# A stream of converted weights in an attention and gated-MLP kernel: fewer conversion passes, another order of stages, and high halves cast on GpSimd

## The chip, the cores and the metric

One core of a Trainium2 chip runs the whole kernel in one launch. The core has TensorE (matmuls, with a weight load that overlaps them), VectorE (DVE), ScalarE (ACT), GpSimd (POOL), a queue of DMA issues on SyncE (SP) and 16 DMA engines. The metric is the device time of an execution in microseconds. The kernel before takes 1339.32 us, the median of three runs (1336.44 to 1340.88).

## The reference

The weights are float64; the kernel reads them as pairs of 32-bit words and makes one float32 of each pair. The other inputs are float32. B, H, S, D are 4, 12, 448, 64; the model width is 768; the two MLPs have widths 1536 and 2048.

```
q_n, k_n = rmsnorm(q, g_q), rmsnorm(k, g_k)
attn = softmax(q_n @ k_n.T / sqrt(64))        # 48 heads of 448 x 448
x = (attn @ v), heads side by side            # 1792 x 768
x = ((x @ w_a) * (x @ w_b)) @ w_out           # 768 -> 1536 -> 768
h = x @ w_in                                  # 768 -> 2048
out = (max(h, 0) + alpha * min(h, 0)) @ w_out2   # 2048 -> 768
```

## The kernel before

**Four batches, four kinds of stage.** For each batch b there are the stages a (the two products with w_a and w_b and their elementwise product), y (w_out of the first MLP), h (w_in of the second, then the leaky activation) and o (w_out of the second, transposed back and stored). Activations lie transposed, features on partitions, 448 columns of a batch. Their order is a list (L584); before, it is `a0 y0 a1 y1 h0 o0 h1 o1 a2 y2 h2 a3 o2 y3 h3 o3`. Every value is kept as a sum of two float16 numbers, a high and a low half, and a product of two such values is three matmuls (`prod`, L725). A unit of weights is 768 x 128 (for o 512 x 128) and serves 18 (12) matmuls; one stage is 24 units for a, 12 for y, 16 for h and 24 for o.

**The weight stream.** `stream` (L599) lists the units in the order of use. At its first use a unit is loaded raw (`w_load`, 768 KB), made float32 (`w_convert`), scaled by a power of two that comes from a sum of squares over its chain (`w_scale`, a small matmul with ones adds over partitions), split into halves (`w_split`) and written to scratch in device memory; later uses reload the halves (384 KB). After each unit, `next_w` calls `advance`, which lets each of these steps run so many units ahead of the one in use: 9, 7, 7 and 3 before (L692), 4 for reloads. `w_convert` is one ScalarE pass and three or four VectorE passes; `w_split` is a ScalarE cast for the high half (L684) and a VectorE pass for the low half (L685). There are 76 first uses in all; 8 conversions and 4 splits are done before a0.

**Attention, woven in.** A step (`att_steps`, L536) makes scores, softmax and probabilities of two tiles of 128 rows; seven tiles make a pair of heads, six pairs a batch, 21 steps a batch. Batch 0 is worked before a0, in float32. Later batches use halves: `probs` (L464) casts the high half on ScalarE (L477), makes the low half on VectorE (L478) into a `p16` buffer and transposes both by DMA (L484); `pv` multiplies with v. `RATE` (L883) says how many steps fall into each stage; a stage a(b) begins when its batch's steps are done. A stage that is followed at once by the one that reads its result (`after`, L781) splits its outputs at its end; otherwise the splits become tasks, one a unit.

**Order.** The framework orders each engine's instructions by a planner's costs, with a few pinned to the order of the program; each engine then runs its list in order, and waits at an instruction whose inputs are not there. DMAs are issued in order by SP. PSUM for stage products has three buffers (`ps_m`).

Of the kernel before, what the change touches and what calls it, by code (L numbers as in the profile page):

```python
# [19 lines left out]
def attention_gated_mlps_kernel(  # L20
# [57 lines left out]
    k16 = acts.tile([KP, 2, 2 * KB, 2, D], F16, name="k16")  # L78
    p16 = [acts.tile([128, 2, KB, 128], F16, name=f"p16_{i}") for i in range(3)]
    stat = [acts.tile([128, 2, NI + 2 * KB], F32, name=f"stat{i}") for i in range(2)]  # L80
# [11 lines left out]
    al = const.tile([128, KF2], F32, name="al")  # L92
    alb = const.tile([128, KF2], F32, name="alb")
    cg = const.tile([128, 1], F32, name="cg")
    icg = const.tile([128, 1], F32, name="icg")
    ncg = const.tile([128, 1], F32, name="ncg")
    ssv = const.tile([KP, B, NP], F32, name="ssv")
# [63 lines left out]
    def setup2():  # L161
        nc.gpsimd.dma_start(out=gbc, in_=g_q.rearrange("(o d) -> o d", o=1).broadcast_to([128, D]))
        nc.gpsimd.dma_start(out=gkb, in_=g_k.rearrange("(o d) -> o d", o=1).broadcast_to([128, D]))
        nc.gpsimd.dma_start(out=al, in_=alpha.rearrange("(f p) -> p f", p=128))
        nc.gpsimd.tensor_scalar(al, al, -1.0, None, op0=ALU.mult)

# [17 lines left out]
    def setup4():  # L184

        q = sm_p.tile([128, KF2], F32, tag="al2", name="al2")
        nc.vector.tensor_tensor(q, al, al, op=ALU.mult)
        m = sm_p.tile([128, 1], F32, tag="alm", name="alm")
        nc.vector.tensor_reduce(out=m, in_=q, axis=AX.X, op=ALU.max)
        t = total(m, 1)  # L190
        one = sm_p.tile([128, 1], F32, tag="alm", name="alo")
        nc.vector.tensor_scalar(one, t, 1.0, None, op0=ALU.max)
        power(one, cg, icg)
        nc.vector.tensor_scalar(cg, cg, 2.0 ** -31, None, op0=ALU.mult)
        nc.vector.tensor_scalar(ncg, cg, -1.0, None, op0=ALU.mult)
        nc.vector.tensor_scalar(icg, icg, 2.0 ** 31, None, op0=ALU.mult)
# [164 lines left out]
    def load_vn(b, p):  # L361
        vn = one_p.tile([KP, 2, KB, D], F32, tag="vn", name="vn")
        nc.sync.dma_start(
# [100 lines left out]
    def probs(m):  # L464
# [7 lines left out]
        for j in range(2):  # L472
# [3 lines left out]
            r = ri[:, j:j + 1]  # L476
            nc.scalar.activation(out=t[:, 0, :, 0:KP], in_=pf, func=AF.Copy, scale=r)  # L477
            nc.vector.scalar_tensor_tensor(  # L478
# [104 lines left out]

    stages = "a0 y0 a1 y1 h0 o0 h1 o1 a2 y2 h2 a3 o2 y3 h3 o3".split()  # L584

# [38 lines left out]
    def w_convert(u):  # L624
# [7 lines left out]
        ti = t.bitcast(I32)  # L632
        nc.scalar.activation(out=t, in_=hi.bitcast(F32), func=AF.Abs, scale=2.0 ** -112)  # L633
        i = nc.vector.tensor_scalar(ti, ti, 3, None, op0=ALU.logical_shift_left)
        if u == 0:
            tc.keep_in_program_order(i)
        nc.vector.scalar_tensor_tensor(  # L637
            out=ti, in0=hi, scalar=-0x80000000, in1=ti, op0=ALU.bitwise_and, op1=ALU.bitwise_or
        )
        nc.vector.scalar_tensor_tensor(  # L640
            out=ti, in0=lo, scalar=29, in1=ti, op0=ALU.logical_shift_right, op1=ALU.bitwise_or
        )
        if kind == "o":
# [6 lines left out]
            )  # L650
        wf[u] = t

    def w_scale(u):

        kind, n, part = stream[u]
        if u not in wf:
            return
        _, parts, _ = CHAINS[kind]
        chains = GROUP[kind]
        if part < parts - 1 or n % chains < chains - 1:  # L660
            return
        us = range(u - parts * chains + 1, u + 1)
        ss = sm_p.tile([128, 4], F32, tag="ss", name="ss")[:, 0:len(us)]
        sc = sm_p.tile([128, 2], F32, tag="sc", name="sc")[:, 0:chains]
        for i, x in enumerate(us):
            nc.scalar.activation(  # L666
                out=junk(768, size(kind)), in_=wf[x], func=AF.Square, accum_out=ss[:, i:i + 1]
            )
        power(total(ss, len(us), chains), sc, inv[kind][:, n - chains + 1:n + 1])
        for x in us:  # L670
# [7 lines left out]
    def w_split(u):  # L678
# [4 lines left out]
        w = wh_p.tile([128, 2, 768], F16, tag="w16", name="w16")[:, :, 0:n]  # L683
        nc.scalar.activation(out=w[:, 0], in_=t, func=AF.Copy, scale=s)  # L684
        nc.vector.scalar_tensor_tensor(  # L685
# [5 lines left out]

    STEPS = [(w_load, 9), (w_convert, 7), (w_scale, 7), (w_split, 3)]  # L692
    AGAIN = [(w_load, 4)]
# [127 lines left out]
    def stage_h(b):  # L821
        for f in range(KF2):
# [3 lines left out]
            for kk in range(KD):  # L826
                prod(ps, hw, kk, Y[b, kk], kk == 0, kk == KD - 1)
            next_w()
            t, t2 = tmp(), tmp()
            nc.scalar.activation(out=t, in_=ps, func=AF.Relu, scale=cg)  # L830
            nc.scalar.activation(out=t2, in_=ps, func=AF.Relu, scale=ncg)  # L831
            nc.vector.scalar_tensor_tensor(  # L832
                out=t, in0=t2, scalar=al[:, f:f + 1], in1=t, op0=ALU.mult, op1=ALU.add
            )
            G[b, f] = g = slot(f"g{b}_{f}")
            nc.vector.tensor_copy(g[:, 0], t)
            nc.vector.tensor_tensor(g[:, 1], t, g[:, 0], op=ALU.subtract)
        for kk in range(KD):
# [43 lines left out]

    RATE = {"a0": 15.5, "y0": 8, "a1": 8, "y1": 4, "h0": 3, "o0": 3, "h1": 5, "o1": 5, "a2": 9, "y2": 6, "h2": 9}  # L883

# [82 lines left out]
```

## Time and profile before

| | us |
|---|---|
| median of the runs | 1339.32 |
| profiled execution | 1339.62 |
| its span, first to last instruction | 1337.8 |
| TensorE busy (share) | 1203.4 (90%) |
| VectorE busy | 779.2 (58%) |
| ScalarE busy | 735.2 (55%) |
| GpSimd busy | 12.6 (1%) |
| mean granted TensorE clock | 0.945 of full |

A busy time is the union of an engine's instructions. TensorE's is modelled, since matmuls overlap, so its share does not say how near its peak it is. The engines wait for each other differently from stage to stage, so that the rows below cut the span into stages: each begins with the first matmul of that stage. The DMA share is the mean busy share of the 16 DMA engines. A wait is put down to whatever ended last before the waiting instruction began.

### The profile page before, as it was taken

The page shows a single profiled execution, that of the slowest core. Times are in us where ns is not written, and L with a number is a line of the kernel's source. Part 1 is how long each engine was busy: PE and PEld are TensorE (multiplying, and loading weights), DVE is VectorE, ACT ScalarE, POOL GpSimd, SP SyncE. Part 2 cuts the span into 40 slices and gives each one's busy share as a digit, 9 for nine tenths or more (in the row PEclk, how much of TensorE's full clock was granted, in tenths as well). Part 3 has the DMA queues.
Part 4 walks back from the last instruction along what each step waited for, and adds up shares of the span by engine and source line. Part 5 has one row for each costly group of instructions (what it writes and reads, how often), then busy time and mean ns, then how long its engine had stood idle before and what let it go on. Part 6 is the DMA issues. An engine that isn't in the chain of part 4 may idle for free. (4 is left out here: it accounts for less than half of the span.)

```text
span 1337.8 us, 18305 instructions
## 1 busy us (share of the span) xinstructions
PE 1203.4 (90%) x6574; PEld 611.7 (46%) x6574; DVE 779.2 (58%) x1639; ACT 735.2 (55%) x1480; POOL 12.6 (1%) x33
## 2 busy tenths in 40 slices
PE   6697887667898989988889999998999999999998
PEld 4353343333344545443445554554545555544554
DVE  6788889788888476999968833334045113003510
ACT  6698788778775577976755634444133113013310
POOL 1000000000000000000000000000000000000000
PEclk9798898877898989998999999998999999999999
DMA  4536999997999956967888667765423433543333
GB/s 106 187 103 184 248 260 256 236 252 203 246 259 268 245 144 194 250 200 214 237 222 208 142 158 200 173 158 120 115 95 119 118 112 104 150 125 95 106 117 91
DMA packets 324491, 234.67 MB, mean 175 GB/s; under 512 B 190992, under 2 KB 297744, under 8 KB 324400
## 3 DMA queue, kind: packets, MB, share of 16 engines
q1 hardware_dynamic: 324288, 233.43, 65.8%
q8 instruction: 52, 0.85, 0.3%
q0 software_dynamic: 112, 0.07, 0.1%
q14 instruction: 39, 0.32, 0.1%
HBM read 155.79 MB, written 32.24 MB: 141 GB/s over the span
## 5 line engine op out<-in xcount | busy, mean ns | idle before, releaser
L110 PEld LDWEIGHTS <-w 128*128 128x128 f16 x4896 | 480.8, 100 | 519.7 <-issue 71.0
L110 PE MATMUL p<-x,w 128*128 128x448 f16 x1728 | 347.0, 361 | 16.6 <-DVE w L685 9.6
L110 PE MATMUL p<-g,w 128*128 128x448 f16 x1152 | 232.8, 361 | 15.6 <-ACT w L684 11.6
L110 PE MATMUL p<-y,w 128*128 128x448 f16 x1152 | 224.6, 356 | 3.9 <-ACT y L739 3.6
L110 PE MATMUL p<-ab,w 128*128 128x448 f16 x864 | 172.7, 360 | 6.7 <-ACT ab L739 4.2
L110 PE MATMUL s<-kT,qT 128*64 128x448 f16 (+1 forms) x588 | 109.2, 416 | 26.8 <-ACT pf L434 19.5
L417 DVE TENSOR_REDUCE nm<-s 128x2 f32<-128x896 f32 x84 | 91.2, 1085 | 35.6 <-PE s L110 35.1
L478 DVE SCALAR_TENSOR_TENSOR p<-pf,ri,p 128x448 f16<-128x448 f32 x126 | 83.3, 680 | 42.1 <-ACT p L477 41.9
L477 ACT ACTIVATE p<-pf,ri 128x448 f16<-128x448 f32 x126 | 80.3, 662 | 37.7 <-DMA pT<-p 32.9
L434 ACT ACTIVATE pf<-s,nm,esc 128x448 f32<-128x448 f32 x126 | 90.0, 718 | 2.7 <-DVE p L478 1.0
L761 DVE SCALAR_TENSOR_TENSOR ab<-p,inv_a,t 128x448 f32<-128x448 f32 x48 | 32.6, 679 | 94.0 <-PE p L110 93.7
L857 DVE TENSOR_SCALAR ob<-p,cum 112x512 f32<-112x512 f32 x24 | 18.0, 749 | 116.8 <-PE p L855 108.1
L848 ACT ACTIVATE t<-p,inv_o 128x448 f32<-128x448 f32 x24 | 25.6, 1067 | 107.3 <-PE p L110 107.3
L633 ACT ACTIVATE wf<-raw 128x768 f32<-128x768 f32 (+1 forms) x76 | 63.0, 831 | 37.3 <-DMA raw<-in_moe_w_out_dram 21.9
L830 ACT ACTIVATE t<-p,cg 128x448 f32<-128x448 f32 x64 | 40.3, 629 | 76.2 <-PE p L110 73.6
L832 DVE SCALAR_TENSOR_TENSOR t<-t,al 128x448 f32<-128x448 f32 x64 | 43.6, 681 | 56.1 <-ACT t L831 56.1
L685 DVE SCALAR_TENSOR_TENSOR w<-wf,sc,w 128x768 f16<-128x768 f32 (+1 forms) x76 | 70.2, 926 | 0.3 <-ACT w L684 0.3
L764 ACT ACTIVATE junk<-ab 128x448 bf16<-128x448 f32 x48 | 27.4, 572 | 75.5 <-DVE ab L761 73.2
L666 ACT ACTIVATE junk<-wf 128x768 bf16<-128x768 f32 (+1 forms) x76 | 58.8, 773 | 15.6 <-DVE wf L646 8.9
L684 ACT ACTIVATE w<-wf,sc 128x768 f16<-128x768 f32 (+1 forms) x76 | 63.2, 860 | 6.1 <-DVE sc L120 6.1
L637 DVE SCALAR_TENSOR_TENSOR wf<-raw,wf 128x768 int32<-128x768 int32 (+1 forms) x76 | 65.8, 866 | 0.2
L640 DVE SCALAR_TENSOR_TENSOR wf<-raw,wf 128x768 int32<-128x768 int32 (+1 forms) x76 | 65.8, 866 | 0.2
(134 smaller groups left out, 1080.3 us busy)
## 6 DMA issues: line engine op xcount, KB each, us to landing
w<-sc_a SPq DMA_DIRECT2D x72, 384.0 KB, 3.3
w<-sc_h SPq DMA_DIRECT2D x48, 384.0 KB, 3.1
w<-sc_o SPq DMA_DIRECT2D x72, 256.0 KB, 3.0
w<-sc_y SPq DMA_DIRECT2D x36, 384.0 KB, 3.1
raw<-in_moe_w_in_dram SPq DMA_DIRECT2D x16, 768.0 KB, 6.1
raw<-in_moe_w_out_dram SPq DMA_DIRECT2D x24, 512.0 KB, 3.9
raw<-in_moe_w_a_dram SPq DMA_DIRECT2D x12, 768.0 KB, 5.7
raw<-in_moe_w_b_dram SPq DMA_DIRECT2D x12, 768.0 KB, 5.6
```

The costliest lines, as they stand in the source:

```text
L110: nc.tensor.matmul(out=o, lhsT=a, rhs=b, start=first, stop=last)
L417: nc.vector.tensor_reduce(out=nm, in_=ps[:, :, 0:S], axis=AX.X, op=ALU.max, negate=True)
L434: nc.scalar.activation(out=pf, in_=ps[:, j, 0:S], func=AF.Exp, bias=nm[:, j:j + 1], scale=scale[j], accum_out=su[:, j:j + 1],)
L477: nc.scalar.activation(out=t[:, 0, :, 0:KP], in_=pf, func=AF.Copy, scale=r)
L478: nc.vector.scalar_tensor_tensor(out=t[:, 1, :, 0:KP], in0=pf, scalar=r, in1=t[:, 0, :, 0:KP], op0=ALU.mult, op1=ALU.subtract,)
L633: nc.scalar.activation(out=t, in_=hi.bitcast(F32), func=AF.Abs, scale=2.0 ** -112)
L637: nc.vector.scalar_tensor_tensor(out=ti, in0=hi, scalar=-0x80000000, in1=ti, op0=ALU.bitwise_and, op1=ALU.bitwise_or)
L640: nc.vector.scalar_tensor_tensor(out=ti, in0=lo, scalar=29, in1=ti, op0=ALU.logical_shift_right, op1=ALU.bitwise_or)
L666: nc.scalar.activation(out=junk(768, size(kind)), in_=wf[x], func=AF.Square, accum_out=ss[:, i:i + 1])
L684: nc.scalar.activation(out=w[:, 0], in_=t, func=AF.Copy, scale=s)
L685: nc.vector.scalar_tensor_tensor(out=w[:, 1], in0=t, scalar=s, in1=w[:, 0], op0=ALU.mult, op1=ALU.subtract)
L832: nc.vector.scalar_tensor_tensor(out=t, in0=t2, scalar=al[:, f:f + 1], in1=t, op0=ALU.mult, op1=ALU.add)
```

## The change

The order of stages becomes `a0 y0 h0 o0 a1 y1 a2 h1 o1 y2 a3 h2 y3 o2 h3 o3`, with other rates of attention steps (4 in a0, 14 in a1). `w_convert` takes the sign along in the ScalarE pass (Prelu with a negative slope of a power of two, in place of Abs) and so drops the VectorE pass that joined the sign. The squares of a unit are summed at the end of `w_convert`, and `w_scale` only adds the totals; the lookaheads become 10, 8, 6 and 3. `w_split` and `probs` cast the high half on GpSimd instead of ScalarE; there are four `p16` buffers for three. Stage h uses one Relu on ScalarE and a VectorE pass that reads PSUM again, then the common `split`, in place of two Relus, a VectorE pass, a VectorE copy and a VectorE subtraction. The tile `vn` shares the pool of the output tiles.

```diff
--- before.py
+++ after.py
@@ -76,7 +76,7 @@
     kT0 = [kT0[:, i] for i in range(2)]
     kd0 = acts.tile([128, 2 * KB * D], F32, name="kd0")
     k16 = acts.tile([KP, 2, 2 * KB, 2, D], F16, name="k16")
-    p16 = [acts.tile([128, 2, KB, 128], F16, name=f"p16_{i}") for i in range(3)]
+    p16 = [acts.tile([128, 2, KB, 128], F16, name=f"p16_{i}") for i in range(4)]
     stat = [acts.tile([128, 2, NI + 2 * KB], F32, name=f"stat{i}") for i in range(2)]
 
     ident = const.tile([128, 128], F32, name="ident")
@@ -90,10 +90,8 @@
     gi = const.tile([128, 1], F32, name="gi")
     esc = const.tile([128, 1], F32, name="esc")
     al = const.tile([128, KF2], F32, name="al")
-    alb = const.tile([128, KF2], F32, name="alb")
     cg = const.tile([128, 1], F32, name="cg")
     icg = const.tile([128, 1], F32, name="icg")
-    ncg = const.tile([128, 1], F32, name="ncg")
     ssv = const.tile([KP, B, NP], F32, name="ssv")
     ssab = const.tile([128, 2, KF], F32, name="ssab")
     sx, ix, sab, iab, sy, iy, cum = [
@@ -162,7 +160,6 @@
         nc.gpsimd.dma_start(out=gbc, in_=g_q.rearrange("(o d) -> o d", o=1).broadcast_to([128, D]))
         nc.gpsimd.dma_start(out=gkb, in_=g_k.rearrange("(o d) -> o d", o=1).broadcast_to([128, D]))
         nc.gpsimd.dma_start(out=al, in_=alpha.rearrange("(f p) -> p f", p=128))
-        nc.gpsimd.tensor_scalar(al, al, -1.0, None, op0=ALU.mult)
 
     def setup3():
         tc.keep_in_program_order(
@@ -184,7 +181,7 @@
     def setup4():
 
         q = sm_p.tile([128, KF2], F32, tag="al2", name="al2")
-        nc.vector.tensor_tensor(q, al, al, op=ALU.mult)
+        tc.keep_in_program_order(nc.vector.tensor_tensor(q, al, al, op=ALU.mult))
         m = sm_p.tile([128, 1], F32, tag="alm", name="alm")
         nc.vector.tensor_reduce(out=m, in_=q, axis=AX.X, op=ALU.max)
         t = total(m, 1)
@@ -192,7 +189,7 @@
         nc.vector.tensor_scalar(one, t, 1.0, None, op0=ALU.max)
         power(one, cg, icg)
         nc.vector.tensor_scalar(cg, cg, 2.0 ** -31, None, op0=ALU.mult)
-        nc.vector.tensor_scalar(ncg, cg, -1.0, None, op0=ALU.mult)
+        nc.vector.tensor_scalar(al, al, -1.0, 1.0, op0=ALU.mult, op1=ALU.add)
         nc.vector.tensor_scalar(icg, icg, 2.0 ** 31, None, op0=ALU.mult)
 
 
@@ -359,7 +356,7 @@
         d["qT"], d["kT"] = qT, kT
 
     def load_vn(b, p):
-        vn = one_p.tile([KP, 2, KB, D], F32, tag="vn", name="vn")
+        vn = ob_p.tile([KP, 2, KB, D], F32, tag="ob", name="vn")
         nc.sync.dma_start(
             out=vn, in_=v[b, 2 * p:2 * p + 2].rearrange("h (p i) d -> p h i d", i=KB)
         )
@@ -474,7 +471,7 @@
             t = p16[(2 * m + j) % len(p16)]
             pf = pfs[j].rearrange("p (i j) -> p i j", i=KB)
             r = ri[:, j:j + 1]
-            nc.scalar.activation(out=t[:, 0, :, 0:KP], in_=pf, func=AF.Copy, scale=r)
+            nc.gpsimd.tensor_scalar(t[:, 0, :, 0:KP], pf, r, None, op0=ALU.mult)
             nc.vector.scalar_tensor_tensor(
                 out=t[:, 1, :, 0:KP], in0=pf, scalar=r, in1=t[:, 0, :, 0:KP],
                 op0=ALU.mult, op1=ALU.subtract,
@@ -581,7 +578,7 @@
             yield fin
 
 
-    stages = "a0 y0 a1 y1 h0 o0 h1 o1 a2 y2 h2 a3 o2 y3 h3 o3".split()
+    stages = "a0 y0 h0 o0 a1 y1 a2 h1 o1 y2 a3 h2 y3 o2 h3 o3".split()
 
     CHAINS = {"a": (2 * KF, 1, KD), "y": (KD, 2, KF // 2), "h": (KF2, 1, KD), "o": (KD, 4, KF2 // 4)}
 
@@ -630,13 +627,13 @@
         lo, hi = pair[:, :, 0], pair[:, :, 1]
         t = wf_p.tile([128, 768], F32, tag="wf", name="wf")[:, 0:size(kind)]
         ti = t.bitcast(I32)
-        nc.scalar.activation(out=t, in_=hi.bitcast(F32), func=AF.Abs, scale=2.0 ** -112)
+
+        nc.scalar.activation(
+            out=t, in_=hi.bitcast(F32), func=AF.Prelu, scale=2.0 ** -112, alpha=-(2.0 ** 32)
+        )
         i = nc.vector.tensor_scalar(ti, ti, 3, None, op0=ALU.logical_shift_left)
         if u == 0:
             tc.keep_in_program_order(i)
-        nc.vector.scalar_tensor_tensor(
-            out=ti, in0=hi, scalar=-0x80000000, in1=ti, op0=ALU.bitwise_and, op1=ALU.bitwise_or
-        )
         nc.vector.scalar_tensor_tensor(
             out=ti, in0=lo, scalar=29, in1=ti, op0=ALU.logical_shift_right, op1=ALU.bitwise_or
         )
@@ -649,24 +646,29 @@
                 op=ALU.mult,
             )
         wf[u] = t
+        _, parts, _ = CHAINS[kind]
+        j = (n * parts + part) % (parts * GROUP[kind])
+        if j == 0:
+            sums[0] = sm_p.tile([128, 4], F32, tag="ss", name="ss")
+        nc.scalar.activation(
+            out=junk(768, size(kind)), in_=t, func=AF.Square, accum_out=sums[0][:, j:j + 1]
+        )
+        if j == parts * GROUP[kind] - 1:
+            squares[u] = sums[0][:, 0:j + 1]
+
+    sums, squares = [None], {}
 
     def w_scale(u):
 
+        if u not in squares:
+            return
         kind, n, part = stream[u]
-        if u not in wf:
-            return
         _, parts, _ = CHAINS[kind]
         chains = GROUP[kind]
-        if part < parts - 1 or n % chains < chains - 1:
-            return
         us = range(u - parts * chains + 1, u + 1)
-        ss = sm_p.tile([128, 4], F32, tag="ss", name="ss")[:, 0:len(us)]
         sc = sm_p.tile([128, 2], F32, tag="sc", name="sc")[:, 0:chains]
-        for i, x in enumerate(us):
-            nc.scalar.activation(
-                out=junk(768, size(kind)), in_=wf[x], func=AF.Square, accum_out=ss[:, i:i + 1]
-            )
-        power(total(ss, len(us), chains), sc, inv[kind][:, n - chains + 1:n + 1])
+        iv = inv[kind][:, n - chains + 1:n + 1]
+        power(total(squares.pop(u), len(us), chains), sc, iv)
         for x in us:
             scales[x] = sc[:, (x - us[0]) // parts:(x - us[0]) // parts + 1]
 
@@ -681,7 +683,7 @@
         t, s = wf.pop(u), scales.pop(u)
         n = t.shape[1]
         w = wh_p.tile([128, 2, 768], F16, tag="w16", name="w16")[:, :, 0:n]
-        nc.scalar.activation(out=w[:, 0], in_=t, func=AF.Copy, scale=s)
+        nc.gpsimd.tensor_scalar(w[:, 0], t, s, None, op0=ALU.mult)
         nc.vector.scalar_tensor_tensor(
             out=w[:, 1], in0=t, scalar=s, in1=w[:, 0], op0=ALU.mult, op1=ALU.subtract
         )
@@ -689,7 +691,7 @@
         w16[u] = w
 
 
-    STEPS = [(w_load, 9), (w_convert, 7), (w_scale, 7), (w_split, 3)]
+    STEPS = [(w_load, 10), (w_convert, 8), (w_scale, 6), (w_split, 3)]
     AGAIN = [(w_load, 4)]
     cur = [0]
     seen = set()
@@ -826,15 +828,12 @@
             for kk in range(KD):
                 prod(ps, hw, kk, Y[b, kk], kk == 0, kk == KD - 1)
             next_w()
-            t, t2 = tmp(), tmp()
-            nc.scalar.activation(out=t, in_=ps, func=AF.Relu, scale=cg)
-            nc.scalar.activation(out=t2, in_=ps, func=AF.Relu, scale=ncg)
+            t = tmp()
+            nc.scalar.activation(out=t, in_=ps, func=AF.Relu, scale=-1.0)
             nc.vector.scalar_tensor_tensor(
-                out=t, in0=t2, scalar=al[:, f:f + 1], in1=t, op0=ALU.mult, op1=ALU.add
+                out=t, in0=t, scalar=al[:, f:f + 1], in1=ps, op0=ALU.mult, op1=ALU.add
             )
-            G[b, f] = g = slot(f"g{b}_{f}")
-            nc.vector.tensor_copy(g[:, 0], t)
-            nc.vector.tensor_tensor(g[:, 1], t, g[:, 0], op=ALU.subtract)
+            G[b, f] = split(t, cg, f"g{b}_{f}")
         for kk in range(KD):
             Y.pop((b, kk))
 
@@ -880,7 +879,7 @@
             G.pop((b, f))
 
 
-    RATE = {"a0": 15.5, "y0": 8, "a1": 8, "y1": 4, "h0": 3, "o0": 3, "h1": 5, "o1": 5, "a2": 9, "y2": 6, "h2": 9}
+    RATE = {"a0": 4, "y0": 5, "h0": 4, "o0": 8, "a1": 14, "y1": 7, "a2": 4, "h1": 4, "o1": 8, "y2": 6}
 
     if True:
         load_qk(0)
```

## Rows read from the trace of the kernel before

**Rows 1.** Stages: window, us, busy of PE, PEld, DVE, ACT, POOL, PEclk, DMA, GB/s

```profile
134.10:310.50 176.40, 129.31 (x684) 61.58 (x683) 149.01 (x294) 139.04 (x281) 0.56 (x1) 0.84 0.99 252
310.50:376.70 66.20, 60.28 (x333) 28.18 (x332) 58.06 (x123) 56.54 (x116) 0.27 (x1) 0.92 0.91 221
376.70:489.80 113.10, 104.20 (x586) 51.26 (x586) 77.27 (x167) 67.78 (x149) 2.24 (x4) 0.94 0.93 234
489.80:536.70 46.90, 46.90 (x270) 24.79 (x269) 31.50 (x59) 37.99 (x75) 0.00 (x0) 1.00 0.72 185
536.70:601.40 64.70, 60.46 (x327) 30.14 (x324) 64.31 (x127) 54.01 (x96) 2.02 (x3) 1.00 0.80 227
601.40:695.70 94.30, 78.03 (x387) 37.85 (x388) 82.15 (x172) 62.51 (x132) 0.00 (x0) 0.89 0.78 217
...
927.70:977.10 49.40, 47.21 (x247) 23.55 (x247) 9.50 (x19) 15.23 (x27) 0.42 (x3) 0.95 0.41 108
...
1033.10:1114.90 81.80, 81.80 (x435) 42.31 (x433) 9.23 (x14) 16.14 (x36) 0.00 (x0) 1.00 0.38 110
...
1173.80:1218.30 44.50, 42.33 (x224) 21.72 (x223) 1.75 (x6) 7.98 (x14) 0.39 (x2) 1.00 0.38 118
```

**Rows 2.** Stage a0, VectorE's maximum over scores (L417) alone

```profile
134.10:310.50 176.40, 16.24 (x15) 0.84 0.99 252
```

**Rows 3.** DMA issues in a1: count, KB each, us to landing

```profile
w<-sc_a SPq DMA_DIRECT2D x22, 384.0 KB, 5.0
raw<-in_moe_w_in_dram SPq DMA_DIRECT2D x6, 768.0 KB, 7.0
...
pT<-p SPq DMA_TRANSPOSE x18, 4.5
```

**Rows 4.** DMA issues in a3

```profile
w<-sc_a SPq DMA_DIRECT2D x20, 384.0 KB, 3.1
```

**Rows 5.** By line and shape: count | busy us, mean ns | idle before

```profile
L477 ACT ACTIVATE p<-pf,ri 128x448 f16<-128x448 f32 x126 | 80.3, 662 | 37.7 <-DMA pT<-p 32.9 <-ACT pf L434 2.4 <-issue 1.0
...
L685 DVE SCALAR_TENSOR_TENSOR w<-wf,sc,w 128x768 f16<-128x768 f32 x52 | 52.5, 1010 | 0.3 <-ACT w L684 0.3
...
L637 DVE SCALAR_TENSOR_TENSOR wf<-raw,wf 128x768 int32<-128x768 int32 x52 | 49.5, 951 | 0.2
L684 ACT ACTIVATE w<-wf,sc 128x768 f16<-128x768 f32 x52 | 47.6, 929 | 5.6 <-DVE sc L120 5.6
...
L837 DVE TENSOR_TENSOR g<-t,g 128x448 f16<-128x448 f32 x64 | 39.9, 623 | 1.4
...
L634 DVE TENSOR_SCALAR wf<-wf 128x768 int32<-128x768 int32 x52 | 28.6, 551 | 2.3 <-ACT wf L633 2.2
```

**Rows 6.** GpSimd in order of time: start us, us, operation

```profile
1.75 0.29 POOL masks.py:199 TENSOR_SCALAR_AFFINE_SELECT ident<-ident 128x128 f32<-128x128 f32 x1
1.99 0.84 POOL L146 MEMSET qT<- 128x896 f32 x1
...
380.54 0.47 POOL L812 TENSOR_TENSOR cum<-cum,iy 128x1 f32<-128x1 f32 x1 [69.77 <-DVE r L262]
381.08 0.96 POOL L813 TENSOR_TENSOR cum<-cum,icg 128x1 f32<-128x1 f32 x1
...
976.79 0.19 POOL L813 TENSOR_TENSOR cum<-cum,icg 128x1 f32<-128x1 f32 x1
```

**Rows 7.** VectorE in order of time, at the second of these

```profile
381.04 0.95 DVE L637 SCALAR_TENSOR_TENSOR wf<-raw,wf 128x768 int32<-128x768 int32 x1
```

**Rows 8.** Chain that ended last: start us, us, what

```profile
852.55 0.88 PE s L110 x8
853.43 10.32 PE p L110 x54
...
875.82 2.27 PE x L110 x24
```

**Rows 9.** ScalarE's table loads, by line

```profile
L237 ACT ACT_TABLE_LOAD x1 | 1.3, 1283 | 0.7 <-PEq L951 0.7
```

## The prediction

> **What bounds the kernel now.** I read the stage table first: the span cut where the first matmul of each stage starts. The reader is to see two halves. From h1 on TensorE is busy nearly all the time; a3 [rows 1] takes 81.8 us, and 24 chains of 18 products at 10.32/54 = 0.191 us a product [rows 8] are 82.5. Little is to be had there. In a0, y0, h0 and o0, the stages that convert weights, TensorE is not the limit: a0 lasts 176.4 us for 82.5 us of its own products. Its DMA share is 0.99, VectorE is busy 149.0 us and ScalarE 139.0 [rows 1]. So a0 goes at the pace of the DMA engines with VectorE next; h0 has VectorE at 64.3 of 64.7 us; o0 is near both (0.78 and 82.2 of 94.3). a1 is again near DMA, 0.93.
>
> **Prices of the DMA engines.** They are worked out from these shares, because the change moves no byte less, it only moves them elsewhere. a3: 0.38 x 81.8 = 31 us for 20 reloads of 384 KB and a few more [rows 1, 4], about 1.35 us each. a1: 0.93 x 113.1 = 105 us; 27 such reloads (22 of them the row shown) take 36, 6 raw loads of twice the size about 16, so the 18 probability transposes, 9 attention steps with the q, k, v that belong to them, take 53: 5.9 us a step [rows 1, 3, 4]. a0: 0.99 x 176.4 = 175; 15.5 steps [rows 2] take 91, which leaves 83 for 24 units, 3.5 us a unit (read and write-back); by size 2.35 for one of o.
>
> **The change on VectorE.** Conversion loses one of its passes, 0.951 us (0.63 for o, by size) [rows 5]. In h, three passes (one of them the 0.623 us subtraction [rows 5]) become two; about 0.3 us a tile, 5 us a stage. A step costs VectorE 3.5 us by what is left of a0's 149.0, 5.1 by what is left of a1's 77.3; I take 4.3. A conversion that stays is 0.55 + 0.95 = 1.5, a split 1.0 [rows 5].
> - a0: 149.0 - 24 x 0.95 - 11 steps x 4.3 = 79
> - y0: 58.1 - 4 x 4.3 + 7 conversions and 4 splits more, 14 - 5 lost passes, 5 + their totals, 2 = 52
> - h0: 64.3 + 3 x 4.3 + 5 conversions and 4 splits more, 12 - 11 lost passes, 9 - 5 = 75
> - o0: 82.2 + 2 x 4.3 - 19 lost passes, 12 - 3 conversions and 4 splits that moved forward, 8 = 71
>
> **The change on GpSimd.** It gets 72 weight casts and 42 probability casts in these four stages, and no GpSimd op of that shape is in the trace. Below: the memset, 0.84 us for 896 elements, 0.94 ns an element, so 0.42, 0.48 and 0.72 us for 448, 512 and 768. Above: the select, 0.29 us for 128 elements with all its cost charged per element, 2.25 ns, so 1.01, 1.15 and 1.73. Start-up is in the 128x1 op, 0.19 us when nothing disturbs it [rows 6]. I take start-up plus the memset's rate: 0.61, 0.67, 0.91, close to what ScalarE takes for them (0.66, 0.93 [rows 5]): 27 us in a0, 17 in y0, 17 in h0, 23 in o0.
>
> These casts are not free for VectorE. The same 128x1 op that takes 0.19 us alone took 0.96 when it began 0.04 us after a two-input VectorE pass, and it ended 0.05 us after that pass did [rows 6, 7]; the seven of them that met such a pass, from a0's end to h0, took 0.47 to 0.96. So GpSimd stood still until VectorE was done. Whether VectorE stands still behind GpSimd the trace cannot show, its GpSimd work being too small: between nothing and the whole cast. About three quarters of VectorE's time in these stages is two-input or plain scalar passes on SBUF, so I take 70% of each cast: 19, 12, 12, 16 us. The Trainium skill, "SBUF — State Buffer", section "Who interferes with whom", says that a VectorE op with two SBUF inputs and a GpSimd op that reads SBUF exclude each other for a whole instruction, and that whichever starts second is blocked. By that rule, with nothing to fill the gaps, each cast would cost VectorE all its length, 25 us more; the limits below would be 108, 72, 92 and 94 and the time 1334. The trace agrees in the one direction, with 0.96 against 0.19, and is silent on the other.
>
> **The sum by stage**, limit of each as the larger of DMA, VectorE with blocking, and TensorE (own products plus 1.53 us a step: 0.88, and 2.27 for 3.5 steps [rows 8]):
> - a0, 4 steps: DMA 24 x 3.5 + 4 x 5.9 = 108; VectorE 98; TensorE 88
> - y0, 5: DMA 72; VectorE 64; TensorE 49
> - h0, 4: DMA 71; VectorE 87; TensorE 61
> - o0, 8: DMA 90 (6 output stores in it); VectorE 87; TensorE 70
>
> Sum 357; with two resources that close I allow 95%: 376, where the four took 401.6: -26. ScalarE is not in it: a0's 139.0 less 24 x 0.93 and 30 x 0.66 is 97, before eleven steps leave. a1 gets 14 steps for 10 and y1 7 for 2: DMA 32 + 83 = 115 and 57, with a little over, 118 and 59, against 113.1 + 46.9: +17. From h1 to the end (642 us) four steps more, +6, of which o1 with 8 steps touches DMA, +4; but a2, y2 and y3 are no longer followed by a stage that needs their sums. y2 takes 49.4 us for 216 products, 41.3, and a last 2.3 of attention, y3 44.5 for 41.3 [rows 1]: 5.8 and 3.2 are waits at the end and the lower clock (0.95 of full in y2) after them. These go, with about 1 in each stage behind them and 3 at a2's end (estimates): -14. Together -4. Before a0 a conversion pass less, a cast moved, one conversion more: -2, an estimate. The totals (squares moved ahead of the matmul that adds them) lie in stages whose limit is elsewhere: 0. The longer hold of PSUM in h by a second reader: 0, three buffers and VectorE below its limit there; without that cover 16 x 0.3 = 5 in h0. Sum -15 on the profiled 1339.6 us (span 1337.8 and 1.8 around it), the median being 1339.3: **1324 us**.
>
> **Rivals.**
> - GpSimd's casts hide whole: VectorE stays at 79, 52, 75, 71; limits 108, 72, 75, 90, at 97% 356, 20 us less: 1304. For it: GpSimd idles now, and only its own waiting is in the trace. Against: that waiting [rows 6].
> - DMA keeps the pace it has on average: in the six stages a0 to o0 it was busy 499 of 562 us; it has the same work after. At that fill those stages gain about 5 us, and, a1 and y1 being in them, with -4 and -2 the kernel stands at 1330 to 1340, say 1335: the change then doesn't do what it says, since engines were relieved that didn't bound. For it: 0.99 in a0. Against: h0 and o0 had room.
> - Slower: the casts cost VectorE more than they took off it. Place: a0 to o0, the two-input passes behind a cast. Price: the upper cast times at 70%, limits 114, 74, 97, 98, at 95% 403: +27, 1351; with all of each cast on VectorE 129, 83, 106, 110, 1398. Between them, nearer the first: 1365. It decides once a cast takes more than about 0.82 us of VectorE on average (limits of 0.95 x (401.6 - 11) = 371, less 277, over 114 casts; I took 59 us).
> - The new activation is not in the table that the exponential uses. Loads cost 1.283 us and there is one in all now [rows 9]; two a conversion would add 62 us to ScalarE in a0, 31, 41 and 41 after: limits 129, 80, 98 and 93 or so, 1377.
>
> **How the numbers follow.** Forecast 0.46 (1305 to 1338), casts hidden 0.12, DMA's pace 0.14, blocked VectorE 0.23, tables 0.05. A measurement of this kernel can tell about 0.3%, 4 us, from no change. Faster: 0.41 of the forecast's 0.46, the 0.12, a third of 0.14: 0.58. Slower: 0.23, 0.05: 0.28. Same: 0.14. The range 1293 to 1370 leaves out part of the hidden casts below and the far ends of blocking and tables above.
>
> **What would show it.** The stage table after: a0 near 113 us with DMA over 0.9; h0 longer than 64.7; a1 and y1 longer; no stall after y2 and y3. In the lines: a weight cast on GpSimd of 0.9 us unblocked, more in the record since its waiting is in it; the two-input passes (0.951 and 1.010 now) longer, if they are blocked in the record too, or else gaps before them. One table load. Wrong would be: casts of 1.5 us and more with VectorE waiting for them, a0 above 125 us, or a DMA share in a0 well under 0.9 while VectorE is full.

## The result and the profile after

The changed kernel takes 1356.22 us, the median of four runs (1351.66 to 1358.44), against 1337.88 for the kernel before in the same rounds. The ratio is 1.0134, with an interval from 1.0096 to 1.0171: slower by 1.3%, where 1324 was forecast. The time lies inside the stated range of 1293 to 1370, but on the slower side, which had been given 0.28. The profiled execution took 1351.66 us, 1349.9 of them its span.

The stages of the kernel after, in the same form as [rows 1]: window, length in us, busy of PE, PEld, DVE, ACT and POOL, then granted clock, DMA share and GB/s. The first line is all that precedes a0; then follow a0, y0, h0, o0, a1, y1; the last two are y2 and y3.

```profile
0.00:115.60 115.60, 90.47 (x552) 51.90 (x553) 101.47 (x300) 99.83 (x224) 17.36 (x21) 0.96 0.62 171
115.60:251.40 135.80, 108.64 (x559) 53.99 (x556) 109.58 (x192) 77.49 (x163) 77.35 (x37) 0.90 0.89 246
251.40:326.20 74.80, 59.06 (x298) 28.62 (x298) 64.25 (x119) 45.93 (x92) 46.54 (x25) 0.84 0.91 245
326.20:396.00 69.80, 65.61 (x338) 32.53 (x337) 63.16 (x110) 45.17 (x92) 36.04 (x19) 0.91 0.90 253
396.00:526.50 130.50, 91.84 (x464) 42.81 (x465) 101.83 (x201) 59.86 (x132) 70.44 (x43) 0.87 0.76 193
526.50:660.50 134.00, 113.38 (x662) 54.77 (x660) 91.68 (x182) 66.74 (x158) 46.55 (x32) 0.91 0.89 205
660.50:717.90 57.40, 52.78 (x308) 25.95 (x308) 37.30 (x75) 29.81 (x64) 18.21 (x13) 0.98 0.77 180
...
947.10:994.40 47.30, 47.30 (x276) 24.32 (x274) 8.43 (x14) 11.24 (x24) 7.40 (x6) 1.00 0.54 139
...
1131.40:1173.20 41.80, 41.80 (x222) 21.62 (x221) 1.36 (x2) 7.95 (x14) 0.00 (x0) 1.00 0.34 101
```

No engine is full in a0 or o0: in a0 VectorE is busy 109.6 of 135.8 us and the DMA share is 0.89, in o0 101.8 of 130.5 and 0.76. Something holds both back. Its place shows in the groups of instructions: line, shape and count, busy us and mean ns of one, then the idle time of the engine before them and what ended it.

```profile
L474 POOL TENSOR_SCALAR p<-pf,ri 128x448 f16<-128x448 f32 x126 | 190.2, 1520 | 370.8 <-ACT pf L431 101.2 <-DMA pT<-p 76.0 <-DVE ri L468 54.2
L686 POOL TENSOR_SCALAR w<-wf,sc 128x768 f16<-128x768 f32 x52 | 126.3, 2436 | 176.5 <-DVE inv_a L121 54.9 <-DVE sc L118 50.7 <-issue 17.2
L686 POOL TENSOR_SCALAR w<-wf,sc 128x512 f16<-128x512 f32 x24 | 41.0, 1721 | 41.8 <-issue 12.0 <-DVE inv_o L121 10.3 <-DVE sc L118 10.0
...
L475 DVE SCALAR_TENSOR_TENSOR p<-pf,ri,p 128x448 f16<-128x448 f32 x126 | 107.8, 857 | 84.0 <-POOL p L474 83.6 <-DMA pT<-p 0.3
L687 DVE SCALAR_TENSOR_TENSOR w<-wf,sc,w 128x768 f16<-128x768 f32 x52 | 63.2, 1216 | 24.7 <-POOL w L686 24.7
L634 DVE TENSOR_SCALAR wf<-wf 128x768 int32<-128x768 int32 x52 | 34.5, 664 | 1.7 <-ACT wf L631 1.4
```

A cast of 448, 512 and 768 columns takes 1.52, 1.72 and 2.44 us on GpSimd; on ScalarE those of 448 and 768 took 0.66 and 0.93 [rows 5]. The pass behind each cast (L475, L687) makes VectorE wait. Before, the wait ahead of the weights' pass was 0.3 us [rows 5] and that ahead of the probabilities' 41.9:

```profile
L478 DVE SCALAR_TENSOR_TENSOR p<-pf,ri,p 128x448 f16<-128x448 f32 x126 | 83.3, 680 | 42.1 <-ACT p L477 41.9
```

Now, in VectorE's waits (us in total, times, longest):

```profile
DVE p L475 <- POOL p L474: 83.6, 96, 3.3
...
DVE w L687 <- POOL w L686: 34.8, 30, 2.5
```

All of the weights' waits lie in the four converting stages, a0 to o0, and of the probabilities' the following. Together they are 60.8 of the 72.1 us in which VectorE stands still there:

```profile
DVE p L475 <- POOL p L474: 26.0, 30, 3.3
```

### The profile page after: what moved, and what is told of

It reads as the page before. It is cut to its first block, busy times and chain, and to the rows that moved or that the text cites. A ratio compares the mean times of both kernels' runs of the same rounds, so it can differ in the third digit from the quotient of the medians.

```text
span 1349.9 us, 18381 instructions
## 1 busy us (share of the span) xinstructions
PE 1200.7 (89%) x6574; PEld 610.2 (45%) x6574; DVE 765.9 (57%) x1500; ACT 614.9 (46%) x1278; POOL 368.0 (27%) x234
## 4 chain that ended last, share of the span: by engine, by line
PE 46%; issue 1%; DMA 1%; ACT 1%; POOL 1%; DVE 1%; SPq 1%; ACTq 0%; POOLq 0%
PE p L108 43%; PE s L108 1%; POOL p L474 1%; DMA pT<-p 1%; PE x L108 1%; PE p L854 1%; ACT pf L431 1%; DVE nm L414 0%; SPq L355 0%; PE norm L108 0%; ACT t L847 0%; DMA kr<-in_k_dram 0%; DVE p L475 0%; SPq L352 0%; ACT nm L427 0%
## 5 line engine op out<-in xcount | busy, mean ns | idle before, releaser
L474 POOL TENSOR_SCALAR p<-pf,ri 128x448 f16<-128x448 f32 x126 | 190.2, 1520 | 370.8 <-ACT pf L431 101.2
L108 PE MATMUL p<-g,w 128*128 128x448 f16 x1152 | 238.6, 365 | 29.1 <-DVE w L687 22.0
L686 POOL TENSOR_SCALAR w<-wf,sc 128x768 f16<-128x768 f32 (+1 forms) x76 | 167.3, 2210 | 218.2 <-DVE sc L118 60.7
L475 DVE SCALAR_TENSOR_TENSOR p<-pf,ri,p 128x448 f16<-128x448 f32 x126 | 107.8, 857 | 84.0 <-POOL p L474 83.6
L108 PE MATMUL s<-kT,qT 128*64 128x448 f16 (+1 forms) x588 | 110.1, 419 | 27.2 <-ACT pf L431 24.9
L687 DVE SCALAR_TENSOR_TENSOR w<-wf,sc,w 128x768 f16<-128x768 f32 (+1 forms) x76 | 86.2, 1134 | 34.8 <-POOL w L686 34.8
L833 DVE SCALAR_TENSOR_TENSOR t<-t,al,p 128x448 f32<-128x448 f32 x64 | 43.4, 678 | 44.2 <-ACT t L832 44.2
L637 DVE SCALAR_TENSOR_TENSOR wf<-raw,wf 128x768 int32<-128x768 int32 (+1 forms) x76 | 67.7, 892 | 0.1
L741 ACT ACTIVATE g<-t,cg 128x448 f16<-128x448 f32 x64 | 42.7, 667 | 49.5 <-DVE t L833 49.4
L742 DVE SCALAR_TENSOR_TENSOR g<-t,cg,g 128x448 f16<-128x448 f32 x64 | 43.6, 681 | 30.3 <-ACT g L741 30.2
```

Source lines behind the costliest of these rows:

```text
L108: nc.tensor.matmul(out=o, lhsT=a, rhs=b, start=first, stop=last)
L474: nc.gpsimd.tensor_scalar(t[:, 0, :, 0:KP], pf, r, None, op0=ALU.mult)
L475: nc.vector.scalar_tensor_tensor(out=t[:, 1, :, 0:KP], in0=pf, scalar=r, in1=t[:, 0, :, 0:KP], op0=ALU.mult, op1=ALU.subtract,)
L637: nc.vector.scalar_tensor_tensor(out=ti, in0=lo, scalar=29, in1=ti, op0=ALU.logical_shift_right, op1=ALU.bitwise_or)
L686: nc.gpsimd.tensor_scalar(w[:, 0], t, s, None, op0=ALU.mult)
L687: nc.vector.scalar_tensor_tensor(out=w[:, 1], in0=t, scalar=s, in1=w[:, 0], op0=ALU.mult, op1=ALU.subtract)
```

## The experiments

**First, parts undone.** The theory: VectorE, which works its list in order, waits at the low-half pass for a cast that takes longer than priced. Its rivals: VectorE and GpSimd block each other on SBUF, as the prediction had it; or the casts are harmless, and the new order or the pace of the DMA engines makes the loss. In e1 both casts of the kernel after go back to ScalarE; in e2 the weights' alone, in e3 the probabilities' alone. e4 is the kernel before with both casts on GpSimd.

```diff
-            nc.gpsimd.tensor_scalar(t[:, 0, :, 0:KP], pf, r, None, op0=ALU.mult)
+            nc.scalar.activation(out=t[:, 0, :, 0:KP], in_=pf, func=AF.Copy, scale=r)
...
-        nc.gpsimd.tensor_scalar(w[:, 0], t, s, None, op0=ALU.mult)
+        nc.scalar.activation(out=w[:, 0], in_=t, func=AF.Copy, scale=s)
```

> The changed kernel with both high-half casts back on ScalarE; all else as changed. Theory A (the casts on GpSimd are the loss: alone they take 1.4 to 2.2 us where 0.61 to 0.91 were reckoned, and VectorE waits or is blocked): it is faster than the kernel before, 1290 to 1315 us, and o0 falls from 130 to about 95 us. Theory B (the new order and the pace of the DMA engines are the loss): 1335 to 1355 us, with o0 and a1 as long as in the changed kernel.

> The changed kernel with only the weight casts back on ScalarE, probabilities still on GpSimd. Theory A: the weight casts are the longer ones (2.2 us) and stand between VectorE's passes in the four stages that convert, so this gets most of the loss back: 1300 to 1325 us. Theory B: 1340 to 1356 us.

> The changed kernel with only the probability casts back on ScalarE, weights still on GpSimd. Theory A: some gain, since 126 casts of 1.4 us go, and most in o0 and a1: 1325 to 1345 us. Theory B: 1340 to 1356 us.

> The kernel before with both casts on GpSimd and nothing else of the change. Theory A: slower than before by 20 to 50 us, 1358 to 1390, as conversion there is also held by VectorE. Theory B: within 6 us of the kernel before, since its first half goes at the pace of the DMA engines.

| | us, median | ratio to before [95%] |
|---|---|---|
| after | 1356.22 | 1.0134 [1.0096, 1.0171] |
| e1, both on ScalarE | 1289.10 | 0.9630 [0.9597, 0.9663] |
| e2, weights on ScalarE | 1303.50 | 0.9733 [0.9701, 0.9766] |
| e3, probabilities on ScalarE | 1322.84 | 0.9884 [0.9856, 0.9913] |
| e4, before, both on GpSimd | 1425.60 | 1.0656 [1.0627, 1.0684] |

The whole loss is the casts: without them on GpSimd the same redesign is 3.7% faster than before. Probabilities alone cost 14 us (1303.5 - 1289.1), weights alone 34, both 67: 19 more than the sum. No run shows why. That GpSimd's casts hold each other up in one queue is a guess: in the kernel after, its probability casts waited 76.0 us for DMA transposes to free a `p16` buffer (above), but e14 below has such waits without the loss. In the kernel before, the same casts on GpSimd cost 87 us, where 20 to 50 were expected. The stages of e1, in the same order from the start to a1:

```profile
0.00:119.00 119.00, 92.83 (x553) 53.84 (x554) 99.01 (x301) 103.88 (x229) 5.70 (x16) 0.93 0.63 166
119.00:232.20 113.20, 99.85 (x558) 50.55 (x556) 95.89 (x196) 100.73 (x199) 0.95 (x1) 0.98 1.04 289
232.20:297.30 65.10, 55.55 (x295) 27.22 (x294) 52.96 (x103) 58.62 (x112) 0.85 (x3) 0.87 1.07 283
297.30:366.20 68.90, 64.24 (x343) 32.52 (x342) 62.45 (x125) 57.81 (x111) 0.00 (x0) 0.93 0.95 266
366.20:470.00 103.80, 85.10 (x467) 40.14 (x465) 89.53 (x198) 80.98 (x173) 0.00 (x0) 0.92 0.92 236
470.00:601.00 131.00, 114.96 (x665) 55.46 (x663) 84.42 (x180) 83.22 (x189) 0.19 (x1) 0.93 0.95 213
```

a0 is 22.6 us shorter than in the kernel after, y0 9.7, h0 0.9, o0 26.7: 60 of the 62.3 us between the two profiles. ScalarE is busier by 23 us in a0 and does not bind, and the DMA engines move 289 GB/s. So the loss is neither the order's nor the DMA engines'. VectorE's waits in these four stages of e1 are mostly for ScalarE's first pass of the conversion, and 6.5 us for casts:

```profile
DVE wf L634 <- ACT wf L631: 26.3, 20, 4.5
...
DVE w L687 <- ACT w L686: 4.6, 8, 1.2
...
DVE p L475 <- ACT p L474: 1.9, 3, 1.5
```

**Then waiting or blocking, and the gain's source.** e5 is e1, and GpSimd repeats each cast into a tile that nothing reads: the traffic stays and VectorE's wait for its result goes. e6 computes nothing of the kernel; it runs GpSimd's casts and VectorE's passes alone and side by side. e8 is the kernel before with only the new `stages` and `RATE`, e9 is e1 with the old ones.

```diff
 # e5, in w_split (and the same in probs, into shp)
         nc.scalar.activation(out=w[:, 0], in_=t, func=AF.Copy, scale=s)
+        nc.gpsimd.tensor_scalar(shw[:, 0:n], t, s, None, op0=ALU.mult)
 # e9
-    stages = "a0 y0 h0 o0 a1 y1 a2 h1 o1 y2 a3 h2 y3 o2 h3 o3".split()
+    stages = "a0 y0 a1 y1 h0 o0 h1 o1 a2 y2 h2 a3 o2 y3 h3 o3".split()
```

> The changed kernel with both casts on ScalarE, and GpSimd doing each of the 202 casts a second time into a tile that nobody reads. The kernel with the casts on ScalarE took 1289 us, with GpSimd's in the chain 1356. Theory L (the loss is VectorE blocked while GpSimd reads SBUF): most of the 67 us is back, 1320 to 1350 us, and the split passes of VectorE are as long as in the changed kernel (1.2 us for 768 columns). Theory C (the loss is the wait of VectorE and the weight chain for a cast of 1.4 to 2.2 us instead of 0.66 to 0.93): within 10 us of 1289, though VectorE's passes may lengthen.

> Nothing of the reference is computed: GpSimd casts of 128x768 and of 4 x 112 columns, and one without a change of type, 16 of each alone; then VectorE's two-input pass, its pass with one input from PSUM and its shift alone; then the cast of 768 columns together with each of the three. Expected alone: 2.2 us, 1.4 us, and about as long with float32 out (if it is the arithmetic) or about 0.9 us (if it is the change of type). Theory L: with the two-input pass and with the shift, the time of both is near the sum of their times alone; with the PSUM pass each takes as long as alone. Theory C: all three pairs run side by side.

> The kernel before with only the order of stages and the rates of attention steps changed. If the order is what gains (theory of the prediction: -26 in the four converting stages with a lighter VectorE, +17 in a1 and y1, -4 after), alone and with the old conversion it gains little or loses: VectorE keeps 0.95 us a unit more there, so 1330 to 1355 us. If order does it all: about 1290.

> The changed kernel with the casts on ScalarE and with the old order of stages and the old rates: conversion, totals and stage h alone. If a0 is bound by the DMA engines (share 0.99) as the prediction says, the lighter VectorE gains little there: 1315 to 1335 us. If VectorE and ScalarE were the limit: about 1295.

e5: 1297.34 us, 0.9671 [0.9636, 0.9705], some 5 us above e1 by the ratios, with intervals that overlap. Its GpSimd works as much as that of the kernel after (its weight casts of 768 take 2718 ns each), and nearly all of the 67 us are gone. Its stages a0, y0, h0 and o0:

```profile
119.00:236.80 117.80, 102.92 (x559) 52.03 (x558) 103.14 (x196) 101.81 (x199) 90.07 (x36) 0.95 1.01 279
236.80:302.80 66.00, 54.73 (x296) 27.15 (x296) 59.48 (x103) 59.30 (x112) 52.02 (x27) 0.89 1.06 285
302.80:370.60 67.80, 63.70 (x344) 32.18 (x342) 66.33 (x122) 56.65 (x108) 37.79 (x16) 0.95 0.95 260
370.60:481.50 110.90, 86.03 (x466) 40.32 (x465) 98.63 (x201) 84.12 (x178) 87.49 (x44) 0.92 0.89 227
```

| a0 to o0, us | length | VectorE busy | VectorE waiting for casts |
|---|---|---|---|
| e1 | 351.0 | 300.8 | 6.5 |
| e5 | 362.5 | 327.6 | 3.0 |
| after | 410.9 | 338.8 | 60.8 |

In these stages VectorE's passes get longer beside GpSimd in e5 too, by 27 us in all against 38 in the kernel after, and that costs 11.5 us. The other 48 us come only where VectorE waits for the casts. So it is mainly the wait for the result and in a smaller part the traffic; what the last 11 us of longer passes would cost without the wait, no run shows. The timeline of e6 gives the sizes (start us, us, engine, operation, count):

```profile
4.90 36.64 POOL L63 TENSOR_SCALAR pw<-a,gate 128x768 f16<-128x768 f32 x16 [2.31 <-DVE gate L56]
42.21 23.84 POOL L66 TENSOR_SCALAR pb<-a,gate 128x448 f16<-128x448 f32 x16 [0.67 <-DVE gate L94]
66.53 36.63 POOL L70 TENSOR_SCALAR pm<-a,gate 128x768 f32<-128x768 f32 x16 [0.48 <-DVE gate L94]
103.39 16.83 DVE L73 SCALAR_TENSOR_TENSOR lo<-d,gate,hi 128x768 f16<-128x768 f32 x16
120.70 11.48 DVE L77 SCALAR_TENSOR_TENSOR e<-ps,gate,d 128x448 f32<-128x448 f32 x16
132.54 6.81 DVE L81 TENSOR_SCALAR e<-d 128x448 int32<-128x448 int32 x16
139.84 58.90 DVE L73 SCALAR_TENSOR_TENSOR lo<-d,gate,hi 128x768 f16<-128x768 f32 x48
139.90 42.47 POOL L63 TENSOR_SCALAR pw<-a,gate 128x768 f16<-128x768 f32 x16 [36.74 <-DVE gate L97]
199.23 46.03 DVE L77 SCALAR_TENSOR_TENSOR e<-ps,gate,d 128x448 f32<-128x448 f32 x64
199.36 36.64 POOL L63 TENSOR_SCALAR pw<-a,gate 128x768 f16<-128x768 f32 x16 [16.99 <-DVE gate L97]
245.62 44.42 DVE L81 TENSOR_SCALAR e<-d 128x448 int32<-128x448 int32 x64
245.87 37.50 POOL L63 TENSOR_SCALAR pw<-a,gate 128x768 f16<-128x768 f32 x16 [9.87 <-DVE gate L97]
```

Undisturbed, a cast of 768 takes 36.64/16 = 2.29 us, one of 448 1.49. Side by side, 48 two-input passes took 58.90 us where 48 alone would take 50.5 (3 x 16.83): 8.4 us for 16 casts, 0.53 each, a quarter of a cast and not 70%. The pass with an operand in PSUM lost nothing (46.03 against 4 x 11.48 = 45.9). So neither expectation came out whole: the pairs neither exclude each other nor all run free.

e8: 1349.58, 1.0057 [1.0038, 1.0076]; e9: 1287.72, 0.9597 [0.9579, 0.9616]. The new order by itself gains nothing, it loses 0.6%; the cheaper conversion, with what else the kernel after changes besides order and casts, gives all 54 us (1341.68 - 1287.72, both on this chip), where 1315 to 1335 had been expected if the DMA engines bound a0.

**Slack, and what precedes a0.** If the wait is the price, room between cast and pass might cancel it. e10 is the kernel after with the weights' low-half pass one unit and the probabilities' one step behind the cast (with six buffers for `pf` instead of four); e13 is the same with the casts on ScalarE. e11 is the kernel before with `vn` in the output tiles' pool, which has two buffers. e12 is e9 with h2 after a3 and o2 after y3, so that h2 and h3 no longer come right behind y2 and y3, whose sums they need.

```diff
 # e10 and e13
-    STEPS = [(w_load, 10), (w_convert, 8), (w_scale, 6), (w_split, 3)]
+    STEPS = [(w_load, 10), (w_convert, 8), (w_scale, 6), (w_cast, 4), (w_low, 3)]
 # e11
-        vn = one_p.tile([KP, 2, KB, D], F32, tag="vn", name="vn")
+        vn = ob_p.tile([KP, 2, KB, D], F32, tag="ob", name="vn")
 # e12
-    stages = "a0 y0 a1 y1 h0 o0 h1 o1 a2 y2 h2 a3 o2 y3 h3 o3".split()
+    stages = "a0 y0 a1 y1 h0 o0 h1 o1 a2 y2 a3 h2 y3 o2 h3 o3".split()
```

> The changed kernel, casts on GpSimd as there, but each low-half pass of VectorE is put one unit (weights) or one attention step (probabilities) behind its cast in the program, with six buffers for the exponentials in place of four. Theory C (the loss is the in-order wait of VectorE and of the weight chain for a long cast; the shadow casts cost only 8 us): most of the 67 us comes back, 1295 to 1315 us, and VectorE's idle time ended by GpSimd falls from 84 and 35 us to under 40 in all. Theory L (blocked passes): no better than 1340 us.

> Control for the run before: the same late low halves and buffers with both casts on ScalarE. Theory C: VectorE waited little there, so within 10 us of 1289. If it is faster than the late low halves with GpSimd by more than 15 us, occupation and contention of GpSimd still cost something that lateness does not hide.

> The kernel before with one line of the change: the tile vn takes two buffers of the output pool in place of one of its own. In the kernel before SP waits 27 us for the squares that free vn, and the loads of q and k queue behind it; TensorE waits 8.8 us for kd there. If that is what shortened the part ahead of a0 (134 us to 116 to 119 in every kernel with the change): 1322 to 1330 us, with a0 beginning near 120. If it was the lighter conversion: within 4 us of the kernel before.

> The conversion of the change with casts on ScalarE and the old order and rates up to y2, then y2 a3 h2 y3 o2 h3 o3: only y2 and y3 no longer come right ahead of the stage that reads them. The old order took 1288 us. By the prediction's step for these waits: 5.8 + 3.2 us and about 1 in the stage behind each, so about 11 us less, 1277. If the waits turn up elsewhere: 1285 to 1290.

e10: 1340.98, 0.9978 [0.9957, 0.9998]; e13: 1288.02, 0.9596 [0.9560, 0.9632]. The slack gives back some 21 of the 67 us by the ratios, where 41 or more were expected, and e13, level with e1, shows that the slack itself costs nothing. VectorE's waits in e10 hardly fell, from 118.4 us to 113.9:

```profile
DVE p L482 <- POOL p L474: 62.6, 68, 3.7
...
DVE w L703 <- POOL w L694: 51.3, 34, 3.5
```

A likely reason stands in GpSimd's own waits in e10, where the probability cast waits for a `p16` buffer that a transpose holds; that it waits longer because the pass is later was not shown:

```profile
POOL p L474 <- DMA pT<-p: 194.8, 21, 43.5
```

So this experiment did not remove the wait that it was to remove, and decides little. e11: 1332.12, 0.9912 [0.9880, 0.9944]; a0 begins at 122.2 us, 11.9 earlier than before. So some 12 of the 54 us that conversion and small edits gained are this one line's; the other edits (conversion, totals, lookaheads, stage h, the fourth `p16` buffer) were not separated. e12: 1281.31, 0.9539 [0.9505, 0.9572], 6 us under e9 by median and 8 by ratio, where 11 were expected.

**A dose of GpSimd.** The kernel after, with only the first quarter (e14) or half (e15) of each cast's columns on GpSimd and the rest on ScalarE; every pass still needs a cast on GpSimd, and only the shares of the two engines differ. e16 is e12 with the quarter.

```diff
-        nc.gpsimd.tensor_scalar(w[:, 0], t, s, None, op0=ALU.mult)
+        h = n // 4
+        nc.gpsimd.tensor_scalar(w[:, 0, 0:h], t[:, 0:h], s, None, op0=ALU.mult)
+        nc.scalar.activation(out=w[:, 0, h:n], in_=t[:, h:n], func=AF.Copy, scale=s)
```

> The changed kernel with each cast divided by columns: the first quarter on GpSimd (alone about 0.27 + 192 x 2.5 ns = 0.76 us of 768 columns, 0.55 of 448), the rest on ScalarE. GpSimd keeps its 202 casts and its queue. If the length of the cast that VectorE waits for is the loss: VectorE's idle time ended by casts falls from 118 us to about 40 and the time to 1283 to 1297 us. If it is GpSimd's in-order queue (a cast that waits for its buffer holds the next ones): 1310 us or more, since the queue is as it was.

> The same with half the columns on GpSimd: about 1.24 us and 0.85 us alone, against 0.93 and 0.66 on ScalarE whole. If length is the loss, between the quarter and the whole and nearer the quarter: 1292 to 1315 us. If the queue: as the quarter, 1310 or more, or as the whole, 1356.

> The fastest kernel so far (conversion of the change, casts on ScalarE, old order with y2 a3 h2 y3 o2 h3 o3 at its end: 1281 us) with a quarter of each cast on GpSimd. ScalarE, busy 0.85 to 0.9 of a0 and y0, gets some 27 us less: 1272 to 1282 us if ScalarE is near the limit there; 1281 to 1290 if contention with VectorE takes it back.

| share on GpSimd | us | ratio to before [95%] | VectorE's waits for casts at the two low-half passes, us |
|---|---|---|---|
| none (e1) | 1289.10 | 0.9630 [0.9597, 0.9663] | 39.6 |
| quarter (e14) | 1290.54 | 0.9639 [0.9599, 0.9678] | 39 |
| half (e15) | 1302.57 | 0.9730 [0.9698, 0.9761] | 56 |
| weights on ScalarE (e2) | 1303.50 | 0.9733 [0.9701, 0.9766] | 79.3 |
| probabilities on ScalarE (e3) | 1322.84 | 0.9884 [0.9856, 0.9913] | 85.9 |
| all (after) | 1356.22 | 1.0134 [1.0096, 1.0171] | 118.4 |

The longest of these waits in e1 (its 4.6 us at L687 are shown above), then those of e14, then of e15:

```profile
DVE p L475 <- ACT p L474: 35.0, 41, 2.9
...
DVE p L476 <- POOL p L474: 27.3, 34, 2.2
...
DVE w L690 <- POOL w L688: 5.8, 9, 1.0
...
DVE p L476 <- POOL p L474: 40.9, 43, 3.1
...
DVE w L690 <- POOL w L688: 9.9, 11, 1.1
```

Time goes with the wait on the whole: without more of it (e14) there is no loss, and with most of it the largest. It is not one for one: from e1 to e2 the wait rises by 39.7 us and the time by 14; from e1 to e3 by 46.3 and 34; and e15 is as slow as e2 with 23 us less of it. Why a late weight is dearer than a late probability stays open. TensorE's own waits for weights do not show it: those that end with a cast or a low half of the weights are 29.0 us in the kernel after and 11.7 in e1, but in e3 only 14.8.

The quarter also speaks against GpSimd's queue as a cause by itself. In e14 its probability casts waited for DMA transposes longer than in the kernel after, 111.2 us against 76.0, and no time is lost:

```profile
L474 POOL TENSOR_SCALAR p<-pf,ri 128x112 f16<-128x112 f32 x126 | 89.3, 717 | 439.0 <-ACT pf L431 125.4 <-DMA pT<-p 111.2 <-DVE ri L468 87.8
```

e16: 1280.28, 0.9559 [0.9525, 0.9594], no better than e12: relieving ScalarE buys nothing. The fastest by its ratio is e12, the cheaper conversion with ScalarE's casts in an order that differs from the old one in two places.

## Why the prediction was wrong

**The step that failed** is in "The change on GpSimd": "I take start-up plus the memset's rate: 0.61, 0.67, 0.91". In e6 the casts of 448 and 768 take 1.49 and 2.29 us undisturbed: above even the upper bound of 1.01 and 1.73, which the select gave. The price came from a memset, which reads no operand, at 0.94 ns an element; the casts take 2.5. It isn't the change of type: with float32 written the cast takes the same 2.29 us. With it failed the term that the sum doesn't have: VectorE's wait for a cast's result, put at nothing, was 60.8 us in the four stages. The prediction had named these signs itself: casts of 1.5 us and more with VectorE waiting for them, and a0, at 135.8 us, above 125.

**The mechanism was the lesser one of two.** The prediction charged VectorE 70% of each cast for blocking, 59 us in four stages. It is blocked, by 38 us there; over the whole kernel L475 took 857 ns against 680 before, L687 1216 against 1010 [rows 5], L634 664 against 551 [rows 5]. That VectorE's busy time came out as forecast, 338.8 us against the 336 that its four VectorE sums with blocking make, is luck: without blocking it is 300.8 in e1, where 277 had been forecast. What the forecast lacked is idle time. The step to 376 allowed 40 us of it, and there were 72. The next instruction of VectorE needs the cast's result, so that the pass and all conversion work behind it stand still for what is left of the cast. On ScalarE that costs little in these stages, 6.5 of the 39.6 us of e1's waits. The section of the Trainium skill that the prediction weighed ("SBUF — State Buffer", "Who interferes with whom") is borne out for one pair: in e6 the pass with an operand in PSUM is free. But there the two-input pass and the casts end 58.90 us after they begin together, where full exclusion would need 50.5 + 36.6 = 87.1: here the measurement decides, and the exclusion is partial. Nothing in the prediction asked what a slow producer does to an engine that works in order; its rival "slower" had the place and, at 1351 to 1398, the size, but for the reason of blocking alone, so that its number is right by luck in part.

**Stage by stage**, in us:

| | before | forecast | after | e1 |
|---|---|---|---|---|
| ahead of a0 | 134.1 | 132 | 115.6 | 119.0 |
| a0, y0, h0, o0 | 401.6 | 376 | 410.9 | 351.0 |
| a1, y1 | 160.0 | 177 | 191.4 | 187.2 |
| from a2 (before: h1) | 642.1 | 638 | 632.0 | 630.4 |

- The four stages: 35 us over the forecast, through the casts. With them on ScalarE, e1's 351.0 are near the 356 that the prediction had for casts that cost VectorE nothing.
- DMA: "a0 goes at the pace of the DMA engines" took a share of 0.99 at 252 GB/s [rows 1] for a ceiling. e1 shows 1.04 at 289 GB/s in a0 and 1.07 at 283 in y0. The prices worked out from the shares were no limits: e9's a0 did 19 attention steps, 24 x 3.5 + 19 x 5.9 = 196 us at these prices, in 167.8, and e1's y0 took 65.1 where 72 was the limit.
- What the change gains: the prediction looked for it in the four converting stages, out of which the new order takes attention steps. Order alone (e8) gains nothing, conversion and the small edits alone (e9) 54 us. By stage, e9's profile is 16.3 us shorter ahead of a0, 8.6 in a0 (with 19 attention steps in it for 15), 13.2 in o0, and 1 to 4 in y0, a1, y1 and h0 each.
- "Before a0 ... -2": the kernel after gained 18.5. e11 shows 11.9 of it to be the line that gives `vn` a second buffer, an edit that the prediction left without a price. TensorE's wait there for `kd` is 4.5 us in e11, 11.5 before.
- a1 and y1: "+17" was forecast and +31 came. a1 took 134.0 us where 118 was forecast. It did 16 attention steps, not 14, which at the prediction's 5.9 us is 12 of the 16 us over; but y1, with 5 steps instead of 7, was not shorter for it (57.4 against 59). Some 4 us of the two stages are the casts; the rest is in e1 too, with a DMA share of 0.95 in a1. Nothing was run to separate DMA from the attention steps: this stays open.
- a2, y2 and y3: the waits in y2 and y3 went, as forecast. TensorE is busy throughout and the granted clock 1.00 in both. y3 fell from 44.5 [rows 1] to 41.8; y2 fell only from 49.4 [rows 1] to 47.3, because 29 more matmuls of attention lie in it (276 against 247). From a2 on the kernel after needed 10 us less than before from h1 on, where 4 less were forecast.
- Tables: one load, of 1283 ns, as before [rows 9]; that rival is out. So is the one in which the DMA engines keep their average pace (e1 is 46 us under its 1335), and so is "casts hide whole", the casts having cost 67. The price of the rival on tables was mis-summed: its limits add up to 400, at 95% 421, which gives 1369 and not 1377.

## What to carry to other kernels

Price work on a new engine from a row of the same kind of instruction, operands included, or leave the range as wide as the rows make it; here a memset gave a cast 0.91 us that took 2.29. Then ask who needs the result: where the next instruction of an engine that works in order is its consumer, the producer's length can be on the path however idle the producer was. Moving work off an engine that does not bind gained nothing here (ScalarE), even at the best dose. A change of many parts is judged by its parts: this one held a gain of 54 us and a loss of 67.

## What was not expected of the hardware

- GpSimd's cast from float32 with one scalar per partition takes 2.5 ns an element in e6 ((2.29 - 1.49) us over 320 elements) and 0.37 us besides. ScalarE's 768 took 929 ns [rows 5].
- VectorE's plain shift loses more beside GpSimd than the two-input pass: 64 took 44.42 us where 4 x 6.81 = 27.2 are undisturbed, while the casts took 37.50 instead of 36.64.
- The mean busy share of the DMA engines can be over 1 in a stretch, and a share of 0.99 was no ceiling: a0 ran at 0.99 and 252 GB/s before, and at 1.05 and 264 GB/s in e11, which is the kernel before but for one line. The 289 GB/s of e1's a0 came with fewer attention steps in it (6 against 15).
